# A memory-augmented recurrent transformer with a gated MLP: moving the left lines' mix, the staged pieces and the left stores

## The chip, the cores and the metric

One NeuronCore of a Trainium2 chip runs the whole kernel. The metric is the device time of one execution in microseconds, as the median of several runs.

## The reference

A sequence of 2048 tokens of width 640 is cut into 64 segments of 32 tokens. Each segment is attended together with 8 memory rows by 32 heads of width 192, and the first 8 rows of its output are the memory of the next segment, so the segments form a chain. A gated MLP over all tokens is independent of that chain, and a gate per token mixes both.

```python
for s in range(n_seg):
    h = concat([mem, x[:, s*32:(s+1)*32]])           # 8 + 32 rows
    q, k, v = h @ Wq, h @ Wk, h @ Wv                 # 32 heads of 192
    scores = where(mask, q @ k.T * scale, -1e9)      # mask: row is memory, or key not after row
    o = (softmax(scores) @ v) @ Wo
    mem = o[:, :8]
    outs.append(o[:, 8:])
a = concat(outs)
b = (gelu(x @ w_gate) * (x @ w_up)) @ w_down
g = sigmoid((x * gate_w).sum(-1, keepdims=True))
return g * a + (1 - g) * b
```

## The kernel before

The MLP comes first, for all tokens; its result goes to a scratch in DRAM. Then the 64 segments run one after the other. The weights Wq, Wk, Wv and Wo don't all fit in SBUF: most pieces stay there, and 16 slots (13 of the projections, of 384 KB, and 3 of Wo, of 480 KB) are swapped in every segment. The swap loads (`load_piece`, L624) are issued by SyncE as soon as the matmuls that read the old piece are done, and even and odd segments run through the octets of heads in opposite order, so that what was loaded last is used first.

Of a segment's 40 rows, 32 are handled directly: the 8 memory rows and the first 24 tokens. The last 8 tokens of a segment don't influence the next memory except as keys and values; these are the "left" lines. They are computed for four segments at a time, 32 rows, one group ahead: `left_mm` projects them, `left_evac` brings Q and K through ScalarE (L919) and VectorE (L921) into rows that a store puts into a scratch in DRAM. Each segment fetches its part of that scratch in two pieces of two octets (`stg_load`, L965), and GpSimd fills them into the Q and K tiles (`left_fill`, L971, L973).

Four segments are a group, and q = s % 4 is the segment's place in it; the text calls q = 0 the first place and q = 3 the fourth. The order of the work is a hand-written list per place: `PROG` for the first three places, `PROG3` for the fourth. Its items are projection steps ("g"), transposes of rows ("tq", "tk"), scores ("sc"), softmax ("ex"), transposes of probabilities ("pt"), the product with V ("pv"), the output projection ("wo"), and in the fourth place the left V of the next group's first octet ("vb"). Items of left work are "lf" (matmuls) and "le" (evacuation). Each instruction is appended to its engine's stream in the order of the list; each engine runs its stream in that order and waits on semaphores, which a scheduler (`_Sched`) derives from the regions that an operation reads and writes.

In the first three places only the direct rows go through Wo (`wo_part`, L1253 and L1278). U, the attention's output, lies in two buffers `uT`, and its left lines are put aside in `uTl`. In the fourth place `wo_both` (L1296) puts 64 rows through Wo at once, from a tile U3 that lies over the `uT` buffers: 32 rows of the segment itself and the 32 left lines of the group, which GpSimd copies from `uTl` into U3 (L1231). Their sum is in the PSUM bank `LB`.

The mix with the MLP has two halves. For the segment's own rows, `mix` scales the MLP rows by 1 - g on GpSimd (L1002, L1007) and adds g times the attention on VectorE (L1009). For the left lines of a group, `mix_left_b` does the first half on GpSimd (L1002, L1015) and `left_sums` the second on VectorE, four instructions that read `LB` (L1345). The result leaves by `outl_store` (L994), eight small stores in the first place of the next group; eight small loads (L983) bring the MLP's left rows in the third place. The segment's own rows leave by L988 and come by L977.

In the next group's first place the bank `LB` takes Q of octet 2 (item ("g", 2, 0)) and then left V of other octets.

The staged pieces lie in `stg`: the first in a buffer of its own, the second over the tail of `uT`, behind the 1536 bytes of U3:

```python
    wsB["uT"] = al(12 * 64 * 2 + 2 * 2 * 2 * LW)
    stg_off = (wsB_off["stg"], wsB_off["uT"] + 1536)
```

A `uT` buffer has 960 bytes, so the second one reaches from 960 to 1920 and overlaps the second staged piece. Its load is issued after the last output projection item.

All DMAs named here are issued by SyncE, in program order, while the segments run. Those of the left lines are `left_store` (L925, 192 KB, one in each of the first three places) and two half stores (L1332) in the second place.

Of the kernel before, what the change touches and what calls it, by code (L numbers as in the profile page):

```python
# [238 lines left out]
def _build(nc, A_x, A_mem0, A_Wq, A_Wk, A_Wv, A_Wo, seg_len, w_gate, w_up, w_down,  # L239
# [49 lines left out]
    def al(n):  # L289
        return (n + 63) // 64 * 64  # L290
# [17 lines left out]
    wsB["v"] = al(NVB * 768)  # L308
    wsB["vl"] = al(NOCT * 768)
    wsB["PT"] = al((8 * R + 8 * 16) * 2)  # L310
    wsB["uT"] = al(12 * 64 * 2 + 2 * 2 * 2 * LW)
    wsB["Qz"] = al(4 * R * 2)
    wsB["p"] = al(4 * 64 * 2)
    wsB["uTl"] = al(NCH * XA * 2)
# [81 lines left out]
    r_Kl = sreg(wsB_off["K"] + 8, 12 * R * 2 - 8)  # L396
    rows_sb = [bview(wsB_off["rows"] + b * 768, 768) for b in range(2)]
    r_rows = [sreg(wsB_off["rows"] + b * 768, 768) for b in range(2)]
    stg_off = (wsB_off["stg"], wsB_off["uT"] + 1536)
    assert NUB == 2 and 24 * R < 1536 < 48 * R <= wsB["uT"]  # L400
    stg = [bview(b, 8 * LW).rearrange("p (o m c i) -> p o m c i", m=2, c=12, i=M) for b in stg_off]
    stg_half = [bview(b, 8 * LW) for b in stg_off]
    stg_flat = stg_half[0]
# [185 lines left out]
    o = 0  # L589
# [331 lines left out]
        S_.add("dve", lambda e: e.transpose(out=dst.rearrange("p q c i -> p c q i"), in_=rowl.rearrange("p (c r) -> p c r", r=L)),  # L921
               reads=[r_rowl], writes=rd, name="L T%s g%d o%d" % ("qk"[m], g, o))

    def left_store(g, o, b):
        S_.add(AUXQ, lambda e: e.dma_start(  # L925
            qkl[4 * g:4 * g + 4].rearrange("s p c -> p s c")[:, :, 2 * LW * o:2 * LW * (o + 1)], lst_rows[b]),
            reads=[r_lst[b]], writes=[Rg("qk", NSEG * o + 4 * g, NSEG * o + 4 * g + 4)], dma_sem="lst%d" % b,
            name="lst store g%d o%d" % (g, o))
# [333 lines left out]
    def half_sums(bank, tag):  # L1262
        for h in (1, 0):
            S_.add("dve", lambda e, h=h: e.tensor_tensor(
                out=zsum[64 * h:64 * h + 64], in0=ps[0:64, bank, DJ * h:DJ * (h + 1)], in1=zpart[0:64, DJ * h:DJ * (h + 1)],
                op=ALU.add), reads=[r_ps[bank], r_zp], writes=[r_zp], name="Zs " + tag)
# [58 lines left out]
    def left_evac(s, u, m):  # L1325
        g, o = unit(s, u)
        bk = lb.pop((u, m))
        if (s % 4, u) in mids:
            dst, rd = ((v_sb[1], [r_v[1]]), (stg_flat, r_stg))[m]
            d4 = dst.rearrange("p (q c i) -> p q c i", q=4, i=M)  # L1330
            left_rows(g, o, m, bk, d4, rd, rows_sb[1], r_rows[1])
            S_.add(AUXQ, lambda e: e.dma_start(  # L1332
                qkl[4 * g:4 * g + 4].rearrange("s p c -> p s c")[:, :, LW * (2 * o + m):LW * (2 * o + m + 1)],
                dst.rearrange("p (q w) -> p q w", q=4)),
                reads=rd, writes=[Rg("qk", NSEG * o + 4 * g, NSEG * o + 4 * g + 4, 64 * m, 64 * m + 64)], dma_sem="lsm%d" % m,
                name="lst store g%d o%d m%d" % (g, o, m))
            return
        left_rows(g, o, m, bk, lst[3][:, :, m], [r_lst[3]], rowl[m], r_rowl[m])
        if m:
            left_store(g, o, 3)  # L1340

    def left_sums(g):
        for j in range(4):
# [6 lines left out]
    def segment(s):  # L1350
# [3 lines left out]
        for n, item in enumerate(PROGS[q]):  # L1354
            kind, i = item[0], item[1]
            if kind == "g":
                if n == 0:
                    left_fill(s, 0)
                    if s:
                        S_.add("pool", lambda e: e.memset(pl_sb[0:104, :, M * ((q + 3) % 4):M * ((q + 3) % 4) + M], 0.0),  # L1360
                               writes=[r_p], name="pl zero s%d" % s)
                proj(s, item)
                ki = [j for m, j in GROUPS[i] if m == 1 and item[2] == KT - 1]
                kind, i = ("k", ki[0]) if ki else ("", 0)
                if kind == "k" and i == 1:
                    if s > 0:
                        out_store(s - 1)
                    if s + 1 < NSEG:
                        x_load(s + 1)
            elif kind == "tq":  # L1370
                row_transp(s, 0, i)
            elif kind == "tk":
                row_transp(s, 1, i)
            elif kind == "sc":
                scores(s, i)
                if i == 0 and q == 0 and g > 0:
                    left_sums(g - 1)
            elif kind == "ex":
                softmax(s, i)
                if i == NOCT - 1 and s + 1 < NSEG:  # L1380
                    stg_load(s + 1, 0)
            elif kind == "pt":
                p_transp(s, i)
            elif kind == "pv":
                pv_oct(s, i)
                if i == NOCT - 1 and q < 3:
                    half_sums(OB, "s%d" % s)
            elif kind == "lf":
                if i == q and unit(s, item[2]):
                    if item[3] == 0:  # L1390
                        for m in range(2):
                            lb[item[2], m] = misc_bank(s)
                    for m in range(2):
                        LBK[m] = lb[item[2], m]
                    left_mm(*unit(s, item[2]), item[3], unit_piece)
            elif kind == "vb":
                if q == 3 and g + 1 < NG:
                    if i == 0:
                        lb["v"] = misc_bank(s)
                    vl_mm(s + 1, i)  # L1400
            elif kind == "le":
                if i == q and unit(s, item[2]):
                    if n > n_wo:
                        post.append(item[2:])
                    else:
                        left_evac(s, *item[2:])
            else:
                if q == 3:
                    wo_both(s, item)
                else:  # L1410
                    wo_part(s, item)
                if i == 2 and item[2] == 0 and q == 0 and g > 0:
                    outl_store(g - 1)
                if item == ("wo", NOCT - 1, 1) and s + 1 < NSEG:
                    stg_load(s + 1, 1)
            swap_loads(s, item)
            if s == 0 and item == ("g", 0, KT - 1):
                load_residents(3, lambda key: key[0] < 3 and on_tmp(key))
            if s == 0 and item == late_at:
                load_residents(3, lambda key: key[0] == 3)  # L1420
            if n == nqkv:
                bz_load(s)
                if q == 2:
                    bzl_load(g)
                if q == 1 and g + 2 < NG:
                    xl_load(g + 2)
            if n == nqkv and s + 1 < NSEG:
                x_copy(s + 1)
            if n == nqkv and q == 3:
                mix_left_b(g)  # L1430
        kv = [x.rearrange("p (c k) -> p c k", k=KT) for x in (Zt, ps[:, OB2, SC:512], zsum)]
        if q == 3:
            for j in (0, 2, 1, 3):
# [7 lines left out]
        for i in range(2):  # L1441
# [5 lines left out]
            if s + 1 < NSEG:  # L1447
                S_.add("dve", lambda e, ka=ka, kb=kb: e.transpose(  # L1448
                    out=XB4[:, :, ka:kb, XA:L].rearrange("p g k i -> p k g i"), in_=kv[0][:, :, ka:kb].rearrange("p c k -> p k c")),
                    reads=[r_Z[i]] + (r_PTq if q == 3 else []), writes=[r_Hm[i], r_Qm, r_Ql], name="Tm%d s%d" % (i, s))  # L1450
        mix(s)
        if "v" in lb:
            vl_evac(s + 1, octet(s + 1, 0), lb.pop("v"), "act")
        for i in post:
            left_evac(s, *i)
        if s + 1 == NSEG:
            left_sums(g)

    for s in range(NSEG):
        segment(s)  # L1460
# [81 lines left out]
```

## Time and profile before

| | us |
|---|---|
| median of 3 runs | 1750.93 |
| lowest, highest | 1748.39, 1751.14 |
| the profiled execution | 1750.43 |
| its span in the profile | 1748.7 |
| granted TensorE clock in it | 0.995 of full speed |

In the profile L12 is line 12 of the kernel, PE is TensorE's matmuls, PEld its weight loads, DVE VectorE, ACT ScalarE, POOL GpSimd and SP SyncE; a q behind an engine's name stands for its sequencer, which issues DMAs. In a timeline, a row has the start in us, the duration in us (of the merged instructions together), engine, line, operation, tiles and count; the bracket tells how long the engine was idle before it and what ended that. In the table of waits the numbers behind the colon are the total in us, how often, and the longest. An idle time is put down to the last semaphore by the profile.

### The profile page before, as it was taken

To read this page: it belongs to the slowest core of one execution; us is meant where nothing else is said; L and a number is where in the kernel's file an instruction comes from. 1 tells how busy PE (TensorE), PEld (TensorE's weight loads), DVE (VectorE), ACT (ScalarE), POOL (GpSimd) and SP (SyncE) were. 2 spreads that over 40 slices of the span, in tenths; PEclk is the share of its full clock that TensorE was granted. 3 is DMA by queue.
4 is the path that set the end of the run, shared out by engine and by line. 5 is a ranking of instruction groups with operands and counts; after the bars stand their busy time and mean duration, and the time that the engine had idled before them with its cause. 6 is when DMAs were issued, how large, how long until landed. Compare 5 with 4: busy or idle time off the path is not lost.

```text
span 1748.7 us, 75451 instructions
## 1 busy us (share of the span) xinstructions
PE 1598.3 (91%) x37242; PEld 779.9 (45%) x28301; DVE 968.4 (55%) x2918; ACT 783.0 (45%) x1835; POOL 413.6 (24%) x1358
## 2 busy tenths in 40 slices
PE   9999889989998998999999998899999998999987
PEld 4554434344444444444444444444444444444443
DVE  2222655556566565656565665556565665556554
ACT  3222444444454454545444444544444454445443
POOL 1100222222222222222222222222222222222222
PEclk9999999999999999999999999999999999999999
DMA  9914987878788787988888787878888787888886
GB/s 319 316 46 144 337 269 292 306 281 289 286 316 303 272 313 277 325 291 301 285 285 319 257 312 272 312 290 291 284 295 321 284 309 263 305 306 308 291 294 254
DMA packets 272206, 499.27 MB, mean 286 GB/s; under 512 B 106216, under 2 KB 133120, under 8 KB 271872
## 3 DMA queue, kind: packets, MB, share of 16 engines
q1 hardware_dynamic: 268730, 491.34, 79.7%
q8 instruction: 256, 4.19, 1.0%
q10 hardware_dynamic: 3142, 3.09, 0.5%
q14 instruction: 78, 0.64, 0.1%
HBM read 473.22 MB, written 21.11 MB: 283 GB/s over the span
## 4 chain that ended last, share of the span: by engine, by line
PE 39%; DMA 13%; DVE 5%; issue 2%; ACT 2%; POOL 1%; POOLq 0%; SPq 0%; DVEq 0%; ACTq 0%
PE ps L1077 12%; PE ps L226 11%; DMA arena<-in_A_Wv_dram 6%; DMA arena<-in_A_Wo_dram 5%; PE ps L1296 4%; PE ps L1253 3%; DMA arena<-in_A_Wk_dram 3%; PE ps L1217 2%; PE ps L1122 2%; PE ps L914 1%; DVE arena L921 1%; DVE arena L1345 1%; PE ps L1130 1%; PE ps L1278 1%; ACT arena L1100 1%
## 5 line engine op out<-in xcount | busy, mean ns | idle before, releaser
L1077 PE MATMUL ps<-arena 128*32 128x384 bf16 x8660 | 657.3, 330 | 66.6 <-DVE arena L1448 47.9
L226 PE MATMUL ps<-arena 128*32 128x384 bf16 x8960 | 652.2, 328 | 25.6 <-DVE arena L1345 17.9
L1077 PEld LDWEIGHTS ps<-arena 128*32 128x32 bf16 x8660 | 222.8, 96 | 462.6 <-issue 268.2
L1111 DVE STREAM_TRANSPOSE arena<-arena 128x384 bf16<-128x384 bf16 x512 | 274.5, 561 | 153.9 <-ACT arena L1097 153.7
L1097 ACT ACTIVATE arena<-ps 128x384 bf16<-128x384 f32 x512 | 230.4, 492 | 260.8 <-PE ps L1077 249.4
L1235 ACT ACTIVATE arena<-ps 128x480 bf16<-128x480 f32 (+1 forms) x256 | 137.7, 538 | 101.3 <-PE ps L1219 98.5
L1114 POOL COPY arena<-arena 64x160 bf16<-64x160 bf16 x256 | 82.0, 320 | 424.8 <-DVE arena L1111 415.8
L1253 PE MATMUL ps<-arena 128*32 128x320 bf16 x3456 | 178.8, 299 | 2.3 <-ACT arena L1196 0.6
L1100 ACT ACTIVATE arena<-ps 128x384 bf16<-128x384 f32 x256 | 125.0, 488 | 109.5 <-PE ps L1077 107.9
L1202 ACT ACTIVATE arena<-ps 128x448 bf16<-128x448 f32 x192 | 104.7, 545 | 132.1 <-PE ps L1189 132.0
L1149 DVE TENSOR_REDUCE arena<-ps 104x4 f32<-104x160 f32 x256 | 83.0, 324 | 145.5 <-PE ps L1137 145.5
L1161 ACT ACTIVATE ps<-ps 104x160 f32<-104x160 f32 x256 | 75.8, 296 | 141.3 <-DVE ps L1151 139.5
L1163 DVE TENSOR_REDUCE arena<-ps 104x4 f32<-104x160 f32 x256 | 82.5, 322 | 84.5 <-ACT ps L1161 82.7
L971 POOL COPY arena<-arena 128x96 bf16<-128x96 bf16 x256 | 70.5, 275 | 238.1 <-PE ps L1137 157.0
L1296 PE MATMUL ps<-arena 128*64 128x320 bf16 x1536 | 122.7, 302 | 1.1 <-ACT arena L1235 0.9
L1217 PE MATMUL ps<-arena 128*64 128x160 bf16 x1536 | 118.1, 240 | 3.7 <-issue 3.7
L1253 PEld LDWEIGHTS ps<-arena 128*32 128x32 bf16 x3456 | 95.2, 96 | 50.8 <-ACT arena L1196 12.7
L1243 POOL COPY arena<-arena 128x96 bf16<-128x96 bf16 x192 | 51.7, 269 | 273.9 <-ACT arena L1235 266.1
L914 PE MATMUL ps<-arena 128*32 128x384 bf16 x1280 | 107.5, 328 | 0.0
L1219 PE MATMUL ps<-arena 128*64 128x64 bf16 x1536 | 103.5, 193 | 0.3 <-POOL arena L1231 0.3
L1217 PEld LDWEIGHTS ps<-arena 128*64 128x64 bf16 x1536 | 81.4, 109 | 47.4 <-ACT arena L1100 19.7
L1296 PEld LDWEIGHTS ps<-arena 128*64 128x64 bf16 x1536 | 79.2, 109 | 30.9 <-issue 8.5
(93 smaller groups left out, 2160.4 us busy)
## 6 DMA issues: line engine op xcount, KB each, us to landing
arena<-in_A_Wk_dram SPq DMA_DIRECT2D x335, 384.0 KB, 7.0
arena<-in_A_Wv_dram SPq DMA_DIRECT2D x335, 384.0 KB, 9.1
arena<-in_A_Wo_dram SPq DMA_DIRECT2D x205, 480.0 KB, 5.9
arena<-in_A_Wq_dram SPq DMA_DIRECT2D x209, 384.0 KB, 5.4
arena<-left_qk_scratch SPq DMA_DIRECT2D x126, 96.0 KB, 4.2
left_qk_scratch<-arena SPq DMA_DIRECT2D x49, 192.0 KB, 2.3
left_qk_scratch<-arena SPq DMA_DIRECT2D x30, 96.0 KB, 4.8
ffn_b_scratch<-arena ACTq DMA_DIRECT2D x16, 160.0 KB, 4.1
```

What stands on the lines that cost most here:

```text
L226: return e.add_instruction(mybir.InstMatmult(name=nm, start_tensor_calc=like["start"], stop_tensor_calc=stop, tile_size=(128, 32), tile_po ...
L914: fns.append(lambda e, outp=outp, rhs=rhs, j=j: e.matmul(outp, lhs, rhs, start=(k == 0), stop=(k == KT - 1), tile_position=(0, 32 * j)))
L1077: fns.append(lambda e, outp=outp, rhs=rhs, j=j: e.matmul(outp, lhs, rhs, start=(k == 0), stop=(k == KT - 1), tile_position=(0, 32 * j)))
L1097: S_.add("act", lambda e, m=m, bk=bk: e.activation(out=rows_sb[m], in_=ps[:, bk, 0:384], func=ACTF.Copy), reads=[r_ps[bk]], writes=[r_rows ...
L1100: S_.add("act", lambda e, i=i, bk=bk: e.activation(out=v_sb[i % NVB].rearrange("p (c n) -> p c n", c=3), in_=ps[:, bk, 0:384].rearrange("p ...
L1111: S_.add("dve", lambda e: e.transpose(out=dst[:, :, 0:L], in_=rows_sb[m].rearrange("p (c r) -> p c r", r=L)), reads=[r_rows[m]], writes=[r ...
L1202: S_.add("act", lambda e: e.activation(out=PT, in_=ps[:, bank, 0:PTW + 128], func=ACTF.Copy), reads=[r_ps[bank]], writes=[r_PT], name="pT ...
L1217: return [lambda e: e.matmul(full, v[:, e0:e0 + 64], PTm[:, i], start=True, stop=False, tile_position=(0, 64 * i), skip_group_check=True), ...
L1219: lambda e: e.matmul(part, vl[:, e0:e0 + 64], PTl[:, i], start=False, stop=True, tile_position=(0, 64 * i), skip_group_check=True)]
L1235: S_.add("act", lambda e: e.activation(out=apx(u[:, 0, 0, :], [[rs, na], [3 * rs, 4], [1, R]]), in_=ps[:, A, 0:na * W].rearrange("p (c t r ...
L1253: fns.append(lambda e, i=i, t=t, j=j, gv=gv: e.matmul(ps[32 * j:32 * j + 32, bank, 0:2 * DJ].rearrange("p (h n) -> p h n", h=2), lhs2[i], ...
L1296: S_.add("pe", [lambda e, i=i, g_=g_, c=c, p=p: e.matmul(ps[64 * i:64 * i + 64, LB, 0:2 * DJ], U3[:, p % 4, c, :], g_[:, c, 2 * DJ * i:2 * ...
```

## The change

Five places change.

- The second staged piece gets a place of its own behind both `uT` buffers; the region grows by 384 bytes per partition.
- It is loaded right after the product with V of the last octet ("pv", 3) in every place, instead of after the last output projection item.
- `left_sums` of a group is issued at the end of the fourth place, behind `mix`, instead of in the next group's first place, behind the scores of octet 0. For the last group it stays at the end.
- `mix_left_b`, GpSimd's half of it, is issued behind the last "pv" item of the fourth place, and so behind the copy into U3, instead of behind the last projection item.
- The left store of the first three places (`left_store` from `left_evac`) is issued by ScalarE instead of SyncE. The four stores before the segments and the half stores stay on SyncE.

```diff
-    wsB["uT"] = al(12 * 64 * 2 + 2 * 2 * 2 * LW)
+    wsB["uT"] = al(2 * 12 * R * 2 + 2 * 2 * 2 * LW)
...
-    stg_off = (wsB_off["stg"], wsB_off["uT"] + 1536)
-    assert NUB == 2 and 24 * R < 1536 < 48 * R <= wsB["uT"]
+    stg_off = (wsB_off["stg"], wsB_off["uT"] + 48 * R)
+    assert NUB == 2 and 1536 <= 48 * R <= wsB["uT"]
...
-    def left_store(g, o, b):
-        S_.add(AUXQ, lambda e: e.dma_start(
+    def left_store(g, o, b, queue="sp"):
+        S_.add(queue, lambda e: e.dma_start(
...
         if m:
-            left_store(g, o, 3)
+            left_store(g, o, 3, "act")
...
-                if n == 0:
+                if item == ("g", 0, 0):
                     left_fill(s, 0)
...
             elif kind == "sc":
                 scores(s, i)
-                if i == 0 and q == 0 and g > 0:
-                    left_sums(g - 1)
...
                 pv_oct(s, i)
                 if i == NOCT - 1 and q < 3:
                     half_sums(OB, "s%d" % s)
+                elif i == NOCT - 1:
+                    mix_left_b(g)
+                if i == NOCT - 1 and s + 1 < NSEG:
+                    stg_load(s + 1, 1)
...
-                if item == ("wo", NOCT - 1, 1) and s + 1 < NSEG:
-                    stg_load(s + 1, 1)
...
-            if n == nqkv and q == 3:
-                mix_left_b(g)
...
         mix(s)
+        if q == 3:
+            left_sums(g)
...
-        if s + 1 == NSEG:
-            left_sums(g)
```

## The prediction

> **What bounds the kernel now.** I read the page first, then the table of waits, then two segments as windows, then the timeline of single engines around the three places that the change touches.
>
> The page: the profiled execution's span, the busy shares, and the chain that ended last.
>
> ```profile
> span 1748.7 us, 75451 instructions
> PE 1598.3 (91%) x37242; PEld 779.9 (45%) x28301; DVE 968.4 (55%) x2918; ACT 783.0 (45%) x1835; POOL 413.6 (24%) x1358
> PE 39%; DMA 13%; DVE 5%; issue 2%; ACT 2%; POOL 1%; POOLq 0%; SPq 0%; DVEq 0%; ACTq 0%
> ```
>
> TensorE is busy 91% of the time and leads the chain, with DMA second: a kernel of 64 short segments in which TensorE runs nearly without pause, and each pause costs its full length. So I look for who makes TensorE wait. In the waits, the columns are total us, times, and longest:
>
> ```profile
> PE ps L226 <- DVE arena L1345: 17.9, 15, 1.2
> PE ps L1278 <- DMA arena<-in_A_Wo_dram: 12.9, 20, 2.7
> PE ps L1077 <- DMA arena<-in_A_Wk_dram: 8.4, 16, 0.7
> PE ps L1077 <- DMA arena<-in_A_Wv_dram: 7.5, 21, 0.6
> PEld ps L1050 <- POOL arena L1231: 6.2, 15, 0.5
> ```
>
> L1345 is the left lines' mix (four VectorE instructions a group); TensorE waits 1.2 us for it once in each of 15 groups. The next three rows are weights that arrive late, 28.8 us together. The last is the copy of old left lines into U3 (L1231), behind which GpSimd's first half of the left mix stands.
>
> How full the DMA engines are, in a segment of the first place (the first of its group) and one of the third; the last two columns are the share of the 16 engines and GB/s:
>
> ```profile
> 966.79:991.04 24.25, 22.12 (x612) 11.42 (x472) 16.55 (x49) 11.75 (x28) 5.78 (x20) 1.00 0.80 284
> 1016.08:1038.50 22.42, 20.97 (x552) 9.73 (x412) 13.82 (x43) 11.32 (x27) 6.57 (x21) 1.00 0.91 324
> ```
>
> With 0.80 to 0.91 of the engines taken, time saved on TensorE can run into late weights. That is the main doubt below.
>
> **Step 1: the left sums go to the end of the fourth place.** One group's place, in the order PE, DVE, ACT, and the wait of the weight load beside it:
>
> ```profile
> 971.75 0.34 PE L1077 MATMUL ps<-arena 128*32 128x384 bf16 x4
> 973.28 0.49 PE L226 MATMUL ps<-arena 128*32 128x384 bf16 x8 [1.19 <-DVE arena L1345]
> 973.60 0.49 PE L1077 MATMUL ps<-arena 128*32 128x384 bf16 x8
> 971.60 1.63 DVE L1345 SCALAR_TENSOR_TENSOR arena<-ps,arena 32x160 bf16<-32x160 f32 x4
> 972.17 0.49 ACT L1097 ACTIVATE arena<-ps 128x384 bf16<-128x384 f32 x1
> PEld ps L1077 <- ACT arena L1097: 27.8, 16, 1.8
> ```
>
> TensorE has the new V step in its place at 971.75, then wants bank LB for Q of octet 2, which the mix still reads until 973.23. Q and K of that step start at 973.28 and the left V (Vl) at 973.60. The mix stands behind the softmax's max and subtraction of octet 0 on VectorE, so it can't be done sooner where it is. After the change Q starts right behind V, at about 971.91 (half of the 0.34 us row, since steps start 0.16 us apart), K at 972.08, Vl at 972.24. But Vl's bank is that of Q of octet 1, and ScalarE's evacuation of it ends at 972.17 + 0.49 = 972.66; the weight load's wait for L1097 is the sign of it. So Vl starts at about 972.72 instead of 973.60: **0.88 us** a group, not 1.19, and a new wait of some 0.45 us for ScalarE is next. 15 groups: 13.2 us.
>
> What the four instructions cost at the new place, on VectorE at the start of the next segment:
>
> ```profile
> 967.28 0.34 DVE L1009 SCALAR_TENSOR_TENSOR arena<-arena 128x160 bf16<-128x160 bf16 x1
> 969.31 0.58 DVE L1111 STREAM_TRANSPOSE arena<-arena 128x384 bf16<-128x384 bf16 x1 [1.69 <-ACT arena L1097]
> ```
>
> Between the segment's own mix (ends 967.62) and the transpose of the first Q rows (969.31) VectorE is idle for 1.69 us, and the mix takes 1.63. It fits with 0.06 us to spare: nothing. If the own mix came later by x, that transpose and the scores of octet 0 behind it would come later by x, with no cover.
>
> **Step 2: GpSimd's half of the left mix goes behind the copy into U3.** GpSimd, then ScalarE, VectorE and TensorE at the end of a fourth-place segment:
>
> ```profile
> 962.23 0.19 POOL L1002 TENSOR_SCALAR arena<-arena 128x1 f32<-128x1 f32 x1
> 962.71 0.69 POOL L1015 TENSOR_SCALAR arena<-arena 128x160 bf16<-128x160 bf16 x1 [0.28 <-POOL arena L1002]
> 963.46 0.42 POOL L1231 COPY arena<-arena 128x288 bf16<-128x288 bf16 x1
> 964.33 0.69 POOL L1007 TENSOR_SCALAR arena<-arena 128x160 bf16<-128x160 bf16 x1 [0.17 <-POOL arena L1002]
> 963.06 0.44 ACT L1235 ACTIVATE arena<-ps 128x320 bf16<-128x320 f32 x1 [0.73 <-PE ps L1219]
> 963.13 0.32 DVE L1240 CAST arena<-ps 128x160 bf16<-128x160 f32 x1 [2.57 <-PE ps L1219]
> 961.71 1.00 PE L1296 MATMUL ps<-arena 128*64 128x320 bf16 x12
> 962.95 1.33 PE L1050 MATMUL ps<-arena 128*32 128x384 bf16 x12
> 964.21 0.60 PE L1296 MATMUL ps<-arena 128*64 128x320 bf16 x6
> ```
>
> The last output part needs three things: U3's old lines from GpSimd (963.88), the evacuations on ScalarE (963.50) and VectorE (963.45). The copy stands behind the 0.69 us of L1015. With L1015 moved behind it, the copy waits only for the output matmuls that still read U3 (end 962.71), so it runs 962.77 to 963.19, and ScalarE's 963.50 is what is late next. Saved: 0.38 us here; the longest wait in the table's row is 0.5, so I take 0.4, in 15 groups (the last group has no next left V): 6.0 us. The moved pair then delays the segment's own first mix (L1007, 964.33) by some 0.5 us, to 965.5; VectorE wants it at 967.28. Covered by over a microsecond; were that cover gone, it would land on step 1's VectorE order.
>
> **Step 3: SyncE's queue at the segment's end.** SyncE, then TensorE and VectorE, where the first place goes over into the second; below them SyncE and TensorE one segment earlier:
>
> ```profile
> 986.76 5.13 SPq L994 DMA_DIRECT2D out_dram<-arena  x8
> 991.99 0.40 SPq L925 DMA_DIRECT2D left_qk_scratch<-arena  x1
> 992.49 0.46 SPq L965 DMA_DIRECT2D arena<-left_qk_scratch  x1
> 993.00 1.38 SPq L624 DMA_DIRECT2D arena<-in_A_Wk_dram  x1
> 991.35 0.35 PE L1077 MATMUL ps<-arena 128*32 128x384 bf16 x4 [0.68 <-DVE arena L1448]
> 989.68 1.19 DVE L921 STREAM_TRANSPOSE arena<-arena 128x384 bf16<-128x384 bf16 x2
> 967.63 0.33 SPq L624 DMA_DIRECT2D arena<-in_A_Wk_dram  x1
> 967.09 0.35 PE L1077 MATMUL ps<-arena 128*32 128x384 bf16 x4 [0.62 <-DVE arena L1448]
> ```
>
> SyncE issues in order, about half a microsecond each. After eight stores of the left output it still has the left store and the staged piece before the first weight swap, which goes out 1.65 us after TensorE's first matmul (993.00 against 991.35); with a free queue it is 0.54 (967.63 against 967.09). The change takes the store's slot out (991.99 to 992.49) and leaves the staged piece ahead of the swap, behind the eight stores: first swap 0.5 us sooner. Where the second place goes over into the third, SyncE is not so loaded; into the fourth stand eight loads of the same kind instead of the stores. So two crossings a group, 30 of them, times 0.5: 15 us at most, for it counts only where TensorE then waits for weights, and all those waits are 28.8 us. I take 9, between 0 and 15, nearer to the upper end because K, V and Wo waits (57 of them) fall in nearly every segment.
>
> The staged piece itself has its own buffer now and no longer waits for the last output matmuls or U's reads; nobody waits for it in any row of GpSimd's table of waits, so its earlier landing is worth nothing by itself.
>
> On ScalarE the store is a wait for the transpose and one issue:
>
> ```profile
> L925 SPq DMA_DIRECT2D left_qk_scratch<-arena x49: 360/392/1335, 174.0 to 1624.6; - x49
> DMA to landing us min/median/max: 2.1/2.3/7.3
> 993.11 0.87 ACT L1097 ACTIVATE arena<-ps 128x384 bf16<-128x384 f32 x2 [3.07 <-PE ps L1077]
> ```
>
> 49 stores, 4 of them before the segments, so 45 move. VectorE's transposes end at 990.87; ScalarE has nothing to do until 993.11 (idle 3.07 us), so an issue of 0.39 us (median) is free. Without that cover it would be 45 x 0.39 = 18 us.
>
> The row says what SyncE gains per store, 0.4 to 0.5 us. The Trainium skill ("DMA: Bandwidth & Descriptors", section "Issuing engines are not separate DMA queues") says that transfers started by different engines run on the same 16 DMA engines and that a second issuing engine saves only issue time; by that rule step 3 is an issue saving and no bandwidth, at most 45 x 0.4 = 18 us, an estimate near the 15 above.
>
> **The sum.** 13.2 + 6.0 = 19.2 us on TensorE, less a fifth (4 us) given back to weights that are late instead (the engines are up to 0.91 busy), plus 9: 24 us. The profiled execution took 1750.4 us (span 1748.7), the median of the runs is 1750.9; so the median goes to about 1727.
>
> **Rivals.**
>
> *The weights take it back.* TensorE reaches each octet sooner, the swaps can't come sooner. For: 0.91 DMA share, DMA 13% of the chain. Against: in the first place, where step 1 saves, the share is 0.80, so a fifth of the engines' time is free there; and the three weight rows name L1077 and L1278, not L1296, so the fourth place's output, where step 2 saves, isn't held by its weights. Then only step 3's 9 us remain: 1742.
>
> *The staged piece and the ScalarE queue do nothing*, because swaps are bound by the engines and not by their issue. Then 15 us remain: 1736, inside the forecast's range.
>
> *Slower: the store on a second queue gets in the way of the last weights.* On SyncE's queue the store stands behind the Wo pieces. On ScalarE's it may go out while the last Wo piece is on its way, in the first three places, 45 times. The store is 192 KB; at 324 GB/s 0.6 us, at the landing's median 2.3 us at the most; I price it at 0.8, near the bytes. 45 x 0.8 = 36, less 24: 12 us slower, 1763. It decides from about 0.6 us a store. For: the Trainium skill, same page, section "Queues, rings and completion order", says that each DMA engine takes turns between queues packet by packet. No row here shows two queues at once. Against, the last Wo part and the transposes a segment later:
>
> ```profile
> 1015.35 0.39 PE L1278 MATMUL ps<-arena 128*32 128x160 bf16 x12 [0.51 <-DMA arena<-in_A_Wo_dram]
> 1014.32 1.17 DVE L921 STREAM_TRANSPOSE arena<-arena 128x384 bf16<-128x384 bf16 x2
> ```
>
> The transposes end at 1015.49, after the piece has landed and TensorE has gone on, so the store can't be ahead of it there.
>
> **How the numbers follow.** The forecast 0.72 (own range 1715 to 1738, which holds the second rival); the weights take it back 0.13; slower 0.08; nothing measurable 0.03; a gain beyond 36 us, if the swaps' head start removes most of the 28.8, 0.04. The range 1713 to 1742 takes in the first rival and all of step 3's 15 with nothing given back; it leaves out the other three cases, 0.15, and a little of the forecast's own. A measurement of this kernel tells about 0.2%, 3.5 us, from no change. Faster 0.88, same 0.04, slower 0.08.
>
> **What would show it.** L226 no longer waits for the left sums; a wait of 0.4 to 0.5 us for L1097 stands before Vl; the sums run right behind L1009 and the first Q transpose is not later. L1231 ends before the last U evacuation, and TensorE's wait for it is gone. The first swap of the second and fourth places goes out 1.0 to 1.2 us after TensorE's start in place of 1.65; the sum of the Wk, Wv and Wo waits falls below 28.8. I am wrong if these waits grow by what the first two shrink, or if L1278's waits for Wo grow in all of the first three places.

## The result, and the profile after

| | before | after |
|---|---|---|
| median of six runs, us | 1750.12 | 1730.98 |
| lowest, highest | 1742.66, 1754.40 | 1727.56, 1738.19 |
| the profiled execution, its granted clock | 1750.43, 0.995 | 1738.19, 0.992 |

The ratio is 0.9889, with a 95% interval of 0.9855 to 0.9924: the changed kernel is faster by 1.1%, which is 19.4 us by the ratio and 19.1 by the medians. The forecast was 1727, the range 1713 to 1742.

The profiled execution of after is the slowest of its six, and its clock is lower. That matters for every comparison below. Over the 178 timed runs of this study, with one constant for each kernel, the time falls by 1.8 us for each 0.001 of granted clock; among the 72 runs of the kernel before alone it falls by 1.9. With this slope every kernel can be put at a clock of 0.994. There the kernel before takes 1751.2 us and the changed one 1729.9 (standard errors 0.4 and 1.0), a gain of 21.3 us. This text calls that "at equal clock". It leaves out whatever a change does to the clock itself, and in the traces TensorE's pauses lower it (last section); so the table below has the plain ratios beside it.

The page of after, the rows that answer to those of before; then the instruction queue, which the prediction had not looked at:

```profile
span 1736.5 us, 75355 instructions
PE 1596.6 (92%) x37242; PEld 779.2 (45%) x28301; DVE 967.3 (56%) x2918; ACT 782.8 (45%) x1835; POOL 413.9 (24%) x1358
q8 instruction: 256, 4.19, 1.0%
PE 70%; DMA 16%; DVE 7%; ACT 4%; issue 3%; SPq 0%; POOL 0%; DVEq 0%; ACTq 0%; POOLq 0%
```

TensorE's busy time is the same within 2 us (1598.3 before); what fell is its idle time. The table of waits of after (total us, times, longest):

```profile
PE ps L1278 <- DMA arena<-in_A_Wo_dram: 11.5, 18, 1.5
PE ps L1278 <- issue: 9.1, 10, 1.6
PE ps L1217 <- issue: 8.2, 8, 1.4
PE ps L1077 <- DMA arena<-in_A_Wk_dram: 7.1, 11, 2.2
PE ps L1184 <- issue: 5.5, 6, 1.9
PE ps L1077 <- ACT arena L1097: 4.6, 15, 0.3
PE ps L1077 <- DMA arena<-in_A_Wv_dram: 4.5, 14, 0.6
```

L226's 17.9 us for the left sums are gone, and a new wait for ScalarE stands in their place, 0.31 us in each of 15 groups. TensorE's weight load at L1050 no longer waits for GpSimd's copy L1231 (6.2 us before, no such row after). The three weight rows sum to 23.1 us (28.8 before). But there are three rows in which TensorE waits for nothing that the profile names ("issue"); all such idle time of TensorE was 20.5 us before and is 26.2 here. Sums like these differ between executions of one kernel: in the second trace of the changed kernel (e5_full) the weight rows sum to 26.9 us and "issue" to 20.8.

**Step 1 in the timeline**: the same group as in the prediction, first the place of the new V step and left V, then the mix at its new place.

```profile
966.00 0.34 PE L1077 MATMUL ps<-arena 128*32 128x384 bf16 x4
966.16 0.50 PE L226 MATMUL ps<-arena 128*32 128x384 bf16 x8
966.97 0.51 PE L1077 MATMUL ps<-arena 128*32 128x384 bf16 x8 [0.31 <-ACT arena L1097]
966.42 0.88 ACT L1097 ACTIVATE arena<-ps 128x384 bf16<-128x384 f32 x2
961.47 0.34 DVE L1009 SCALAR_TENSOR_TENSOR arena<-arena 128x160 bf16<-128x160 bf16 x1
961.85 1.63 DVE L1345 SCALAR_TENSOR_TENSOR arena<-ps,arena 32x160 bf16<-32x160 f32 x4
963.56 1.04 DVE L1111 STREAM_TRANSPOSE arena<-arena 128x384 bf16<-128x384 bf16 x2
```

V starts at 966.00, Q of octet 2 right behind it, left V at 966.97: 0.97 us, where it was 1.85 (971.75 to 973.60). That is the 0.88 us of the prediction. The mix ends at 963.48 and the first Q transpose starts at 963.56, without an idle time in between; the scores of octet 0 (their first matmul of L1130) start 3.36 us after the segment's first matmul in the mean over the first places (3.34 before).

**Step 2**, GpSimd, ScalarE, VectorE and TensorE at the end of a fourth place:

```profile
957.42 0.43 POOL L1231 COPY arena<-arena 128x288 bf16<-128x288 bf16 x1 [0.71 <-PE ps L1296]
958.32 0.69 POOL L1015 TENSOR_SCALAR arena<-arena 128x160 bf16<-128x160 bf16 x1 [0.19 <-POOL arena L1002]
957.63 0.44 ACT L1235 ACTIVATE arena<-ps 128x320 bf16<-128x320 f32 x1 [0.73 <-PE ps L1219]
957.52 0.94 PE L1050 MATMUL ps<-arena 128*32 128x384 bf16 x12
958.39 1.82 PE L1296 MATMUL ps<-arena 128*64 128x320 bf16 x24
```

The copy ends at 957.85, before ScalarE's evacuation (958.07). The last output part starts 0.81 us after the end of the last product with V in the mean (1.30 before): 0.49 us a group, where I had taken 0.4.

**Step 3**, SyncE, TensorE and ScalarE where the first place goes over into the second, and the left store's own row:

```profile
979.13 5.12 SPq L994 DMA_DIRECT2D out_dram<-arena  x8
984.30 0.41 SPq L965 DMA_DIRECT2D arena<-left_qk_scratch  x1
985.14 0.36 SPq L624 DMA_DIRECT2D arena<-in_A_Wk_dram  x1
984.60 0.35 PE L1077 MATMUL ps<-arena 128*32 128x384 bf16 x4 [1.12 <-DVE arena L1446]
984.16 0.38 ACTq L925 DMA_DIRECT2D left_qk_scratch<-arena  x1
986.36 0.87 ACT L1097 ACTIVATE arena<-ps 128x384 bf16<-128x384 f32 x2 [3.07 <-PE ps L1077]
L925 ACTq DMA_DIRECT2D left_qk_scratch<-arena x45: 366/367/424, 205.1 to 1609.7; - x45
```

The first swap goes out 0.54 us after TensorE's first matmul; it was 1.65 in the segment that the prediction quotes. Over all groups, the means went from 0.93 to 0.54 into the second place and from 1.10 to 0.69 into the fourth. ScalarE's issue lies in an idle time of 3.07 us, as before.

### The profile page after: what moved, and what is told of

The parts are those of the page before. It is cut to its first block, busy times and chain, and to the rows that moved or that the text cites. A ratio compares the mean times of both kernels' runs of the same rounds, so it can differ in the third digit from the quotient of the medians.

```text
span 1736.5 us, 75355 instructions
## 1 busy us (share of the span) xinstructions
PE 1596.6 (92%) x37242; PEld 779.2 (45%) x28301; DVE 967.3 (56%) x2918; ACT 782.8 (45%) x1835; POOL 413.9 (24%) x1358
## 3 DMA queue, kind: packets, MB, share of 16 engines
q8 instruction: 256, 4.19, 1.0%
## 4 chain that ended last, share of the span: by engine, by line
PE 70%; DMA 16%; DVE 7%; ACT 4%; issue 3%; SPq 0%; POOL 0%; DVEq 0%; ACTq 0%; POOLq 0%
PE ps L1077 19%; PE ps L226 17%; DMA arena<-in_A_Wo_dram 6%; PE ps L1296 6%; DMA arena<-in_A_Wv_dram 4%; DMA arena<-in_A_Wk_dram 4%; PE ps L1253 4%; PE ps L1217 3%; PE ps L833 3%; PE ps L830 3%; PE ps L1122 3%; PE ps L914 2%; PE ps L848 2%; DVE arena L921 2%; PE ps L1130 1%
## 5 line engine op out<-in xcount | busy, mean ns | idle before, releaser
L226 PE MATMUL ps<-arena 128*32 128x384 bf16 x8960 | 654.6, 329 | 7.7 <-DVE arena L1044 1.1
L1097 ACT ACTIVATE arena<-ps 128x384 bf16<-128x384 f32 x512 | 230.4, 493 | 259.2 <-PE ps L1077 242.7
L1253 PE MATMUL ps<-arena 128*32 128x320 bf16 x3456 | 178.4, 299 | 2.6 <-ACT arena L1196 1.1
L1217 PE MATMUL ps<-arena 128*64 128x160 bf16 x1536 | 118.2, 240 | 8.2 <-issue 8.2
L1253 PEld LDWEIGHTS ps<-arena 128*32 128x32 bf16 x3456 | 95.8, 96 | 50.6 <-ACT arena L1196 13.1
L1217 PEld LDWEIGHTS ps<-arena 128*64 128x64 bf16 x1536 | 81.7, 109 | 52.1 <-ACT arena L1100 19.7
```

The lines of the kernel that those rows point to most:

```text
L226: return e.add_instruction(mybir.InstMatmult(name=nm, start_tensor_calc=like["start"], stop_tensor_calc=stop, tile_size=(128, 32), tile_po ...
L1097: S_.add("act", lambda e, m=m, bk=bk: e.activation(out=rows_sb[m], in_=ps[:, bk, 0:384], func=ACTF.Copy), reads=[r_ps[bk]], writes=[r_rows ...
L1217: return [lambda e: e.matmul(full, v[:, e0:e0 + 64], PTm[:, i], start=True, stop=False, tile_position=(0, 64 * i), skip_group_check=True), ...
L1253: fns.append(lambda e, i=i, t=t, j=j, gv=gv: e.matmul(ps[32 * j:32 * j + 32, bank, 0:2 * DJ].rearrange("p (h n) -> p h n", h=2), lhs2[i], ...
```

## The experiments

Medians and ratios are from runs beside the kernel before on the same chip; the last column is put at a clock of 0.994 as above, with its standard error in brackets. The runs of e1 to e4, of e5 to e8 with f1 to f3, and of g1 are from three chips; at equal clock the kernel before took 1750.4 to 1751.8 us in all of their series. The two runs of the changed kernel share one value there, as do the two of one other kernel.

| run | what it is | median us | ratio, 95% interval | us at clock 0.994 |
|---|---|---|---|---|
| e1_sums | before + step 1 | 1743.88 | 0.9950 [0.9928, 0.9972] | 1744.5 (1.0) |
| e2_mixb | before + step 2 | 1740.46 | 0.9938 [0.9915, 0.9962] | 1741.4 (1.0) |
| e3_both | before + steps 1 and 2 | 1731.16 | 0.9889 [0.9856, 0.9922] | 1733.7 (1.4) |
| e4_queue | before + step 3 | 1747.51 | 0.9970 [0.9944, 0.9996] | 1745.9 (1.0) |
| e5_full | the changed kernel again | 1731.21 | 0.9891 [0.9857, 0.9925] | 1729.9 (1.0) |
| e6_store_back | changed, left stores on SyncE | 1737.24 | 0.9919 [0.9889, 0.9950] | 1739.0 (0.8) |
| g1_store_back2 | the same again | 1737.28 | 0.9933 [0.9903, 0.9963] | 1739.0 (0.8) |
| f3_no_staged | changed, staged piece as before | 1730.26 | 0.9893 [0.9864, 0.9923] | 1731.4 (1.4) |
| e7_bank | changed, two PSUM banks exchanged | 1729.73 | 0.9871 [0.9833, 0.9909] | 1728.9 (1.4) |
| e8_late | changed, half store of K later | 1734.62 | 0.9906 [0.9874, 0.9939] | 1732.6 (1.0) |
| f1_shift128 | changed, shifted by 128 instructions | 1729.40 | 0.9876 [0.9844, 0.9907] | 1729.7 (1.4) |
| f2_shift64 | e7_bank, shifted by 64 | 1731.88 | 0.9895 [0.9864, 0.9926] | 1733.9 (1.4) |

**e1_sums: step 1 alone.**

```diff
                 scores(s, i)
-                if i == 0 and q == 0 and g > 0:
-                    left_sums(g - 1)
...
         mix(s)
+        if q == 3:
+            left_sums(g)
```

> The kernel before with one part of the change: the left sums at the end of the fourth place. My theory: the wait of L226 for L1345 goes, a wait of about 0.3 us for ScalarE's evacuation stands before left V, 0.88 us a group are won and a fifth given back: 10 to 13 us less than before (ratio 0.9925 to 0.994). Rival, the weights take it back: 0 to 4 us less, with L1077's and L1278's waits for weights up by what is won.

At equal clock 6.7 us faster than before (error of the difference 1.0), less than the 10 to 13 that were expected. In the waits the place itself gave what was costed: L226's 17.9 us became

```profile
PE ps L1077 <- ACT arena L1097: 4.6, 15, 0.3
PE ps L1077 <- DMA arena<-in_A_Wk_dram: 10.8, 21, 0.8
```

13.3 us less, to 0.1 us of the 13.2. About half of it did not reach the end. Where it went isn't shown: in this execution K's weights cost 2.4 us more (8.4 before) and Wq's 1.5 (no row before), but Wo's 2.5 less.

**e2_mixb: step 2 alone.**

```diff
                     half_sums(OB, "s%d" % s)
+                elif i == NOCT - 1:
+                    mix_left_b(g)
...
-            if n == nqkv and q == 3:
-                mix_left_b(g)
```

> The kernel before with one part of the change: GpSimd's half of the left mix behind the copy into U3. My theory: the first output matmul behind the copy starts 0.5 us sooner after the product with V (about 0.8 us behind its end in place of 1.3), 5 to 7 us less than before (0.996 to 0.997). Rival, the weights take it back: no difference, with the next first place's weights late instead.

9.8 us faster at equal clock (1.0), more than the 5 to 7 expected. The place gives 0.49 x 15 = 7.4; the bound that TensorE shows in the kernel before is the weight load's 6.2 us plus 2.0 of the matmuls (L1050 waiting for L1231), at most 8.2, since the two may hold the same time twice. The measured value lies above these by 2.4 and 1.6 us, 2.3 and 1.5 of its errors; what brought the rest isn't shown.

**e3_both: both mixes, step 3 left out** (the two diffs above).

> The kernel before with both moves of the left mix and nothing of the staged piece or the queue. My theory: 15 to 19 us less (0.989 to 0.9915), so that the queue and the staged piece make up the small rest of the change. Rival, the moves only pay together with the sooner swaps: under 8 us less.

17.5 us faster at equal clock (1.4). The parts add: 6.7 + 9.8 = 16.5. So the two mixes bring over four fifths of the gain of 21.3 at equal clock, and by the ratios, 0.9889 for this kernel and for the changed one, all of it.

**e4_queue: step 3 alone**, the left stores on ScalarE's queue and the second staged piece in its own buffer and sooner, as in the change.

```diff
-            left_store(g, o, 3)
+            left_store(g, o, 3, "act")
...
+                if i == NOCT - 1 and s + 1 < NSEG:
+                    stg_load(s + 1, 1)
```

> The kernel before with the other parts only: second staged piece in its own buffer and loaded sooner, left stores on ScalarE's queue. My prediction's step 3: first swap of the second and fourth places 0.4 to 0.5 us sooner, 9 us less, between 0 and 15 (0.991 to 1.0). Rival, swaps are bound by the DMA engines and not by their issue: within 3 us of before, with the weights landing as late as before. Second rival, the second queue gets in the way of the last Wo pieces: slower, with L1278's waits for Wo up.

5.3 us faster at equal clock (1.0). The swaps go out sooner nearly as in the full change (0.63 us after TensorE in the mean, in both places), and in the waits the weights shrink:

```profile
PE ps L1278 <- issue: 15.6, 15, 1.7
PE ps L1278 <- DMA arena<-in_A_Wo_dram: 8.4, 16, 1.3
PE ps L1077 <- DMA arena<-in_A_Wv_dram: 5.6, 14, 0.7
PE ps L1077 <- DMA arena<-in_A_Wk_dram: 3.1, 8, 0.6
```

17.1 us together, 11.7 less than before; but "issue" rises from 20.5 to 25.1, L1278's alone from 12.4 to 15.6. The two together fell by 7.1 us, not far from what the time shows. It looks as if part of what weights no longer cost is waited for without a name; but "issue" differs by 5.4 us between the two traces of the changed kernel, so one trace doesn't show it. What "issue" is, the later runs ask.

**e5_full: the changed kernel again**, beside the next three.

> The changed kernel itself, once more beside the others. Steps 1 and 2 alone took 0.9889 of the time before; if the queue and the staged piece add nothing on top, this is 0.989 again (0.986 to 0.992); if they add their 5 us, 0.986.

1731.21 us against 1730.98 in the first measurement. Against e3_both, step 3 adds 3.8 us (1.7) on top of the mixes at equal clock; the ratios, 0.9889 there and 0.9891 and 0.9889 here, show none. Which of the two is right isn't settled. In this trace the weights sum to 26.9 us (Wk 4.7, Wv 6.3, Wo 15.9) and "issue" to 20.8.

**e6_store_back and g1_store_back2: left stores back on SyncE's queue**, with the rest of the change.

```diff
-            left_store(g, o, 3, "act")
+            left_store(g, o, 3)
```

> The changed kernel with the left stores back on SyncE's queue: both moves of the mix, the staged piece in its own buffer and sooner. Theory, the swaps' head start only turns waits for weights into waits for instructions: the same as the changed kernel within 4 us, first swap of the second and fourth places some 0.2 to 0.4 us later, L1077's waits for weights up by 3 to 6 us and TensorE's idle time with no semaphore behind it down by as much. Rival, the prediction's step 3: 5 to 9 us more than the changed kernel.

> The kernel of the run with the left stores back on SyncE's queue (all else as changed) once more. It was 6 us above the changed kernel, though the run with the mixes alone, which has neither the store's move nor the sooner piece, was not. Theory (the sooner piece in front of a store on SyncE's queue costs something of its own): again 1735 to 1739 us, 0.991 to 0.993 of before. Rival (that job's spread): 1729 to 1734, as the other kernels with both mixes moved.

9.1 us slower than the changed kernel at equal clock (1.3), and also 5.3 slower than e3_both (1.6), which has neither part of step 3. So the theory of the first of these runs, no difference, fell. The second measurement gave the same median. So the sooner staged piece in its own buffer, with the store on the same queue, costs about 5 us, and the store's move gives that back and more. The first swaps still went out sooner than before the change (0.72 us after TensorE into the second place), yet the weights are as late as they were, 29.9 us together, and in the second measurement even later:

```profile
PE ps L1278 <- DMA arena<-in_A_Wo_dram: 12.6, 23, 1.7
PE ps L1077 <- DMA arena<-in_A_Wv_dram: 10.9, 27, 1.1
PE ps L1077 <- DMA arena<-in_A_Wk_dram: 10.0, 20, 0.6
```

33.5 us together. Why the sooner piece makes them late is not settled.

**f3_no_staged: the changed kernel with the staged piece in its old place and buffer**, the stores on ScalarE.

```diff
-                if i == NOCT - 1 and s + 1 < NSEG:
-                    stg_load(s + 1, 1)
...
+                if item == ("wo", NOCT - 1, 1) and s + 1 < NSEG:
+                    stg_load(s + 1, 1)
```

> The changed kernel with the second staged piece loaded where it was before, into the buffer that it shares with the left U; the left stores stay on ScalarE's queue. Theory (the sooner staged piece is worth nothing by itself, the queue is worth little): 1728 to 1734 us, the same as the changed kernel. Rival (the sooner staged piece takes the queue's time when stores stand there too, so that the stores' move is what pays it back, and without the piece the move is a gain): 1724 to 1728. Rival (the staged piece was waited for): 1734 to 1742, with waits for it in the second half of the left U's copies.

Within the errors the same as the changed kernel (1.5 us, error 1.7). The first swaps go out 0.58 and 0.73 us after TensorE, nearly as soon as with the full change: the store's move alone does it. The staged piece and its buffer are worth nothing that can be measured. But the store's move by itself, this kernel against e3_both, gives no more than 2.3 us (1.9): the 9.1 us of the comparison above are in the main the cost of the sooner piece ahead of a store on one queue.

**e7_bank: what is next in the first place.** In the first place the new V step goes to another bank, so that left V waits for V's evacuation and no longer for that of Q of octet 1.

```diff
-bk_of[mi] = LB if s % 4 == 0 and item[1] == 2 and mi[0] == 0 else misc_bank(s, item[1])
+bk_of[mi] = LB if s % 4 == 0 and item[1] == 2 and mi[0] == 0 else OB if s % 4 == 0 and item[1] == 1 and mi[0] == 2 else misc_bank(s, item[1])
```

> The changed kernel with V and Q of the first place's second group exchanged in their banks, so that left V of octet 1 follows V's evacuation (ends 0.38 us sooner) and not Q's. If the 0.3 us wait for L1097 is what is next behind the left sums, it goes (4.6 us over 15 groups) and the kernel takes 2 to 4 us less than the changed one; if TensorE then waits for its instructions or the weights instead, no difference.

The 4.6 us of L1097 are gone from the waits and left V starts 0.59 us after V in place of 0.97; the time fell by 1.0 us at equal clock, with an error of 1.7: no difference. It has the lowest ratio of all that ran, but it can't be told from the changed kernel.

**e8_late: the last Wo piece of the second place sooner.** The half store of K of the left lines goes out behind the last Wo swap, from the second staged buffer.

```diff
-            S_.add(AUXQ, lambda e: e.dma_start(
+            put = lambda: S_.add(AUXQ, lambda e: e.dma_start(
...
+            if item == ("wo", 0, 1):
+                for put in held_stores:
+                    put()
```

> The changed kernel with the second place's half store of K behind the last Wo swap instead of ahead of it, from the second staged buffer, so that the first staged piece no longer waits for it. The last Wo piece of the second place lands 0.3 us sooner; SyncE's wait of 62 us for the half store moves from the first staged piece to the second. Theory, the second place ends with the last Wo piece: 3 to 5 us less than the changed kernel. Rival, instructions or left lines are next: no difference.

No gain where 3 to 5 us were expected: 2.7 us slower than the changed kernel at equal clock, error 1.4. In the waits:

```profile
PE ps L1278 <- issue: 13.7, 13, 1.8
PE ps L1278 <- DMA arena<-in_A_Wo_dram: 7.7, 12, 1.7
```

Wo's row was 11.5 and 15.9 us in the two traces of the changed kernel, L1278's "issue" 9.1 and 8.6. So the weights do come sooner, and the same line has more pauses without a name. But all weights and all "issue" together are 45.2 us here, 49.3 and 47.7 there: these rows don't account for a loss, and why nothing was gained stays open.

**f1_shift128 and f2_shift64: what "issue" is.** The trace of after has 37,242 matmuls and 28,301 weight loads of TensorE; the instruction queue q8 moved 256 packets with 4.19 MB. That is 16,384 bytes a packet and 64 bytes for each of the 65,543 instructions: 256 to a packet. Numbering TensorE's records of e5_full in order of start, its 25 pauses over 0.3 us without a semaphore stand before records 3010, 3266, 7106, 8386, 15042 and so on: 24 of 25 have the remainder 194 by 256, one has 193. In the trace of after it is 175 for 24 and 174 for 2 (a few records are missing there), and the pause ends 1.25 to 1.62 us after the end of a q8 packet, in 26 of 26. The other packet ends fit: in e5_full TensorE never starts the instruction behind one sooner than 1.2 us after the end of a q8 packet, and all 25 pauses are among the 71 ends where it starts within 1.65 us; the 184 ends whose packet came earlier have none. To test it, the instruction stream was moved against the packets:

```diff
+                if a == 0:
+                    S_.add("pe", [lambda e: e.matmul(ps[:, 4, 0:1], ident, ident[:, 0:1], start=True, stop=True)
+                                  for _ in range(64)], reads=[r_ident], writes=[r_ps[4]], name="shift")
```

Here 64 matmuls and their weight loads; in f2_shift64 32, on top of the exchanged banks.

> The changed kernel with 64 extra matmuls of one column (128 instructions with their weight loads) among the first transposes, which shift everything TensorE executes later by half of a 256-instruction packet; what is computed stays the same. In the trace of the changed kernel's second profile each of the 25 idle times of TensorE over 0.3 us that no semaphore ends stands at an instruction whose number in TensorE's own sequence has one and the same remainder by 256. Theory (TensorE waits there for its next packet of instructions): all such idle times move to instructions 128 earlier in the program, so that the lines at which most of them stand (L1217 of the first place, L1278, L1184) change; they again have one remainder; their sum may come out anywhere between 10 and 35 us instead of 21 to 26, and the time follows by about that difference, within 8 us of the changed kernel's, with at most 4 us more for the extra matmuls at the start. Rival (something at those lines delays TensorE): the idle times stay at L1217, L1278 and L1184 with 20 to 26 us, and the time is that of the changed kernel plus 0 to 4 us.

> The changed kernel with V and Q's group exchanged between two PSUM banks in the first place (as in the run with the exchanged banks) and with 32 extra one-column matmuls at the start: a shift by a quarter of a packet. Theory (instruction packets): one remainder again, at instructions 64 earlier than in the run without the shift, other lines than there, a sum of 10 to 35 us, and a time within 8 us of that run's 1729.7. Rival (places in the code): idle times at the same lines as there, about 25 us, and the time 1729.7 plus 0 to 2 us.

All 27 pauses of f1_shift128 again have one remainder, and 34 of 36 in f2_shift64. The lines moved with the shift of 64: f2_shift64 pauses at L1256, L917 and L1125, three lines lower than in the changed kernel's numbering, where every other run shows at most two pauses, all of them at L1253. With the shift of 128 the lines stayed, which I had not expected: lines, sum and time are those that the run's rival named. What tells the two apart is where in time the pauses stand. The trace says why: the pauses at L1217 come every 7,936 records (7106, 15042, 22978 and on), 31 packets, which is two groups; a group is 15.5 packets, so half a packet moves the pause by a group. So it did, from 296.33 and 488.96 us to 198.37 and 390.36, and so for all of that line: 7 pauses in e5_full and 8 in f1_shift128, each in every second group, and never in the same one. The timelines of e5_full, f1_shift128 and f2_shift64, one pause each:

```profile
296.33 0.26 PE L1217 MATMUL ps<-arena 128*64 128x160 bf16 x1 [1.20 <-issue]
```

```profile
390.36 0.26 PE L1220 MATMUL ps<-arena 128*64 128x160 bf16 x1 [1.08 <-issue]
```

```profile
297.96 0.45 PE L1256 MATMUL ps<-arena 128*32 128x320 bf16 x5 [0.59 <-issue]
```

So these pauses are TensorE waiting for its next packet of instructions; shown by both shifts. All "issue" together is 24.4 us in f1_shift128 and 29.2 in f2_shift64. The first takes as long as the changed kernel, the second 5.0 us longer than e7_bank at equal clock (1.9), with 3.6 more of "issue".

## Why the prediction was right

**Step 1** was right in its mechanism and its place: 0.88 us a group, 13.3 us in the waits, and the mix hidden in VectorE's gap. The new wait came out at 0.31 where I had said 0.4 to 0.5: the profile counts it from the end of Q and K's matmuls (966.66), I had counted from the time at which left V could have started. Alone it brought 6.7 us, so half was lost on the way to the end, more than the fifth that I had taken off.

**Step 2** was costed a little low: 0.49 us a group in place of 0.4, 7.4 in place of 6.0, because I chose between one group's 0.38 and the longest 0.5 of the weight load's row. Alone it brought 9.8, of which the place explains 7.4.

**The give-back** of a fifth was about right for the two together: 13.2 + 7.4 = 20.6 us costed with the sizes found, 17.5 measured (1.4), so 3.1 lost. That it fits is partly luck: step 1 alone lost half, and step 2 alone brought more than it was costed.

**Step 3** was the term that was mis-sized: 9 us taken, 5.3 alone (1.0), and on top of the mixes 3.8 at equal clock (1.7) and none by the ratios. Two things were too large. I read the swap's delay, 1.65 us, from one segment; the mean was 0.93 and 1.10, so there were 0.4 us to gain at each of 30 crossings, 12 us and not 15. At the crossing that I quoted the swap came even sooner than the 1.0 to 1.2 us that I had named, at 0.54, because the eight stores ended 0.35 us ahead of TensorE's first matmul there and no longer 0.54 behind it. And I let late weights count as gain once they came sooner. Where TensorE goes on sooner it may meet the next packet of instructions instead: in e4_queue weights fell by 11.7 us while "issue" rose by 4.6, and in the two traces of the changed kernel one is high where the other is low (23.1 and 26.2, 26.9 and 20.8). With such a spread between traces this is not shown. The sign that the prediction named came true, the three weight rows fell below 28.8 (23.1 in the trace of after, 26.9 in e5_full), but it was worth less than the fall, and Wo's row by itself was no smaller in e5_full (15.9, 12.9 before). That the staged piece itself is worth nothing held (f3_no_staged), but only with the store off the queue; in front of it the sooner piece cost about 5 us, which no step foresaw.

The store's landing, 2.3 us in the median before, is in the trace of after

```profile
DMA to landing us min/median/max: 2.1/2.6/7.9
```

so no faster, and what the move gains is the issue slot of the first swap. That is what the Trainium skill says in "DMA: Bandwidth & Descriptors", section "Issuing engines are not separate DMA queues": a second issuing engine saves the time to start a transfer and adds no bandwidth. The trace agrees.

**The sum**: 24 us forecast; 19.4 by the ratio, 21.3 at equal clock. That it came so near is in part luck. With a fifth given back, about 10.6 us of it were step 1, 4.8 step 2 and 9 step 3; alone, at equal clock, the three brought 6.7, 9.8 and 5.3. One term too small made up for much of the two that were too large.

**The rivals.** That the weights take the mixes' gain back (1742) fell: the mixes alone give 17.5 us. That step 3 does nothing (1736) is not ruled out on top of the mixes: of its 9 us, between none and 3.8 are there. Alone it brings 5.3 us. That the store on a second queue delays the last weights (1763) fell with the store's own move: no loss against e3_both (2.3 us faster, 1.9), and a gain of 9.1 us against e6_store_back.

## What to carry to other kernels

When an engine that is nearly always busy stops without a named releaser, count its instructions: pauses that all have one remainder by 256 are instruction packets. Time saved just ahead of such a place may be waited for there; the traces here suggest it and don't show it. Take a delay that is to be multiplied by its count as the mean of all its occurrences, not from the one segment that shows it best. And test parts of a change together as well as alone: two transfers on one queue had a cost of about 5 us that neither the piece's row nor the store's row shows. And before a lower granted clock is taken for chance, look for TensorE's pauses ahead of each stretch at half clock.

## What was not expected of the hardware

- TensorE's instructions come in packets of 16 KB, 256 at a time. At 18 to 34 of the 256 packet ends of a run TensorE stood still for 0.3 to 2.3 us, 17 to 26 us a run; it went on 1.25 to 1.62 us after the packet's record in the profile of after. It stands still where the packet came late; why some come late is not settled. The Trainium skill ("Runtime: NRT & Kernel Launch", section "Instruction fetch mechanics") has the blocks of 16 KB and 256 instructions, and calls the cost of crossing from one to the next mostly hidden. Here about nine ends in ten are hidden; the others cost 1 to 1.5% of the span.
- The granted clock falls where TensorE pauses. In the 14 traces it is full but for the first and last few us and for 64 stretches at half clock, 59 of them of 3.4 us and five two or three times as long; within a trace they start whole multiples of 3.413 us apart. One of them in the trace of after, first the 3.4 us ahead of it, then the stretch itself. A row has the window and its length, the busy time (and count) of TensorE, its weight load, VectorE, ScalarE and GpSimd, then the granted clock, the DMA share and GB/s:

```profile
517.00:520.40 3.40, 1.76 (x56) 0.90 (x48) 2.05 (x6) 1.20 (x3) 0.51 (x3) 1.00 0.55 158
520.40:523.80 3.40, 2.98 (x40) 0.86 (x24) 1.02 (x5) 0.00 (x0) 1.30 (x4) 0.50 0.50 121
```

TensorE is idle for 1.64 us of the first row. Ahead of all 64 stretches it was idle for 1.3 to 2.8 us of the 3.41 us before. Cut into windows of 3.413 us in step with the stretches, the traces (without their first 40 us and their ends) have 42 windows with 1.8 us or more of idle time, and all are followed by half clock; of 42 with 1.6 to 1.8 us 17 are, of 108 with 1.3 to 1.6 us 6, and of 6,198 with less 5, each of these inside a longer stretch. This is read from the traces; no run was made to test it.
- So pauses of TensorE that fall close together cost a second time. A stretch of 3.4 us at half clock loses 1.7 us, and that is 0.001 of the mean clock of a span of 1,730 us: the slope of 1.8 us for 0.001. Over the runs of one kernel, with clocks between 0.987 and 0.998, it accounts for 57% of the variance. Taking it out makes kernels a few us apart easier to compare, but it can also take out a part of what a change does: the mean clock was 0.9938 in 72 runs of the kernel before and 0.9928 in 12 of the changed one, a difference of twice its error.
